# Attention and a SiLU MLP in one kernel: w_in loaded on all partitions, one K in another tag's buffer, a new hand-planned order

## The chip, the cores and the metric

The kernel runs on one core of a Trainium2 chip. The metric is the device time of one execution in microseconds (us). Five runs of the kernel before took 404.73 to 410.91, with a median of 405.35.

Engines are named as the profile names them: PE is TensorE (matmuls; PEld its weight loads), ACT is ScalarE, DVE is VectorE, POOL is GpSimd and SP is SyncE. Here POOL issues all loads, which also turn float32 into float16, and SP and ACT issue the stores.

## The reference

Softmax attention over 8 batches of 12 heads, 448 tokens and 64 dims, and then a two-layer MLP over its 3584 x 768 output:

```python
scores = scale * np.matmul(q, k.transpose(0, 1, 3, 2))
attn = softmax(scores)
attn_out = np.matmul(attn, v)                       # (B, H, S, D)
x = attn_out.transpose(0, 2, 1, 3).reshape(B * S, H * D)
h = x @ w_in                                        # 768 -> 2048
g = h * (1.0 / (1.0 + np.exp(-h)))
return g @ w_out                                    # 2048 -> 768
```

Inputs and output are float32 in DRAM.

## The kernel before

**Units of attention.** A unit is one batch and four heads; batch 0 is cut in two pieces of 224 queries, so that it makes units 0 to 5, and each later batch makes three. For a unit, `load_k` and `load_q` bring K and Q, DVE turns them in 32 x 32 blocks (`turn_k`, `turn_q`), PE computes scores (`s`), ACT takes the exponential (`E`), and PE computes three groups (`a`): the sums of the exponentials (part 0, with weights of ones) and two halves of the output (parts 1 and 2, with V as weights). DVE inverts the sums (`inverse`) and scales the halves into `xT` (`norm`). For most units DVE first adds the first three `E` tiles into a tile `T` (`add_e`), which shortens part 0.

**The MLP.** `ffn1` computes 128 rows of `h` (16 of them to a batch or piece) from six `xT` tiles and `w_in_t`. ACT takes the tanh (`th`), and DVE forms the gated value in `G` or `X` (`gate`). The second layer multiplies 2 x 2 blocks with seven products `p` (Strassen's scheme, with sums on DVE) for 13 "quads" of two 128-row tiles each; the first two tiles use 16 plain matmuls each (`o`). ACT and DVE read the products from PSUM into `ost`, and `store` writes each `ost` tile with four DMAs of 32 rows.

**The dims.** One block of an output half holds, for head `h` of the group, 32 of its 64 dims. Before, half 1 is dims 0 to 31 and half 2 is dims 32 to 63. Row `p` of a `w_in_t` block must hold the matching row of w_in, so `load_w_in` takes 32 partitions of three blocks at a time: 8 loads for each of three column ranges (512, 512 and 1024 columns), 24 in all.

**The order.** Nothing here is scheduled by a framework. The planner at the end of the kernel (`Order`, `Op`, `Ring`) plays through the work with estimated durations and then emits the instructions in that order; every engine runs its own queue in order. A `Ring` stands for a set of buffers: a step is planned only when one is free. On ACT and DVE the planner takes the waiting step with the least ready time plus `bias`, so that a lower bias goes first. On PE a burst of scores is taken when its time has come (`PACE` us after the last one) or when few MLP jobs are queued (`len(moe) < 6`); else an MLP job is taken, and attention groups when they are ready. While no MLP job has run yet, waits on PE are filled with matmuls of zeros (`z`, `run_zeros`).

**Loads.** They stand in POOL's queue in the order of the `plan_*` calls: K and Q of batch 0's three head groups, its V (4 loads), Q of units 3 to 5, the first two quarters of w_in, K and Q of unit 6, the last half of w_in, and so on. K tiles have two buffers (tag `rk`), Q tiles three (`rq`), `T` tiles two. So the third K waits until the first one has been turned.

**Splits.** In batch 0 a burst of scores holds two key chunks. For units below 6 it is split by pairs of heads into two half-bursts, each with its own exponential.

**The last stores.** In the last quad the odd ones of the four stores of a tile go to ACT's queue, but only for the tiles with `i == j` (L584).

Of the kernel before, what the change touches and what calls it, by code (L numbers as in the profile page):

```python
# [9 lines left out]
FP16 = mybir.dt.float16  # L10
# [154 lines left out]
def kernel(  # L165
# [9 lines left out]
    nc = tc.nc  # L175
# [4 lines left out]
    HG = 4  # L180
# [10 lines left out]
    NDC = DM // 128  # L191
    NT = 2 * S // 128
    OH = DM // 2
    PACE = 3
    LONE = NG + 1
    PIECES = ((0, 7), (7, TPP))
    NE, NXT = 9, 16
# [28 lines left out]
    def group_of(src, b, hg):  # L226
        return src[b, HG * hg : HG * (hg + 1)].rearrange("h (i g) d -> (h i) (g d)", g=TPP)

    def load_k(b, hg):
        t = sb.tile([128, TPP, D], FP16, name=f"rk_{b}_{hg}", tag="rk", bufs=2)  # L230
        nc.gpsimd.dma_start(out=t, in_=group_of(k, b, hg))  # L231
        rawk[(b, hg)] = t

# [10 lines left out]

    def load_v(b, hg0, hg1, x):
        if b not in VT:
            VT[b] = sb.tile([128, NH, NCH, D], FP16, name=f"V_{b}", tag="V", bufs=2)
        hs = slice(HG * hg0, HG * hg1)
        first, count = X_TOK[form(b, hg0)][x]
        nc.gpsimd.dma_start(  # L250
            out=VT[b][32 * x : 32 * (x + 1), hs, 0:count, :],
            in_=v[b, hs].rearrange("h (i g) d -> i h g d", g=TPP)[
                :, :, first : first + count, :
            ],
        )


    def load_w_in(h, j, f0, f1):
        src = moe_w_in.rearrange("(c h j p) f -> h j p c f", h=HG, j=2, p=32)
        dst = w_in_t.rearrange("p (c j) f -> p j c f", j=2)  # L260
        nc.gpsimd.dma_start(
            out=dst[32 * h : 32 * (h + 1), j, :, f0:f1], in_=src[h, j, :, :, f0:f1]
        )

    def load_w_out(f0, f1, m0, m1):
# [101 lines left out]
    def attend_mm(a, n, part, c, h, k0, k1, e, start, stop):  # L367
        b, hg, g0, g1 = units[n]
        nq = 32 * (g1 - g0)
        at = nq * (c % per_burst(n))  # L370
        if part == 0:
            w = ones[k0:k1, :]
        else:
            w = VT[b][k0:k1, HG * hg + h, c, 32 * (part - 1) : 32 * part]
        nc.tensor.matmul(  # L375
            out=a[32 * h : 32 * (h + 1), 0:nq],
            lhsT=w,
            rhs=e[k0:k1, h, at : at + nq],
            start=start,
            stop=stop,  # L380
        )
# [193 lines left out]
    def store(qd, i, j):  # L575
        u, t = divmod(2 * qd + i, NT)
        for w in range(4):
            r, col = divmod(128 * t + 32 * w, S)
            b = 2 * u + r
            dst = out[b * S : (b + 1) * S, OH * j : OH * (j + 1)].rearrange(  # L580
                "(i g) m -> g i m", g=TPP
            )

            eng = nc.scalar if w % 2 and 4 * qd + 4 == NT * B and i == j else nc.sync  # L584
            eng.dma_start(
                out=dst[col // 32], in_=ost_t[(qd, i, j)][32 * w : 32 * (w + 1), :]
            )
# [43 lines left out]
    od = Order()  # L631
    s_ring, m_ring, e_ring = Ring(2), Ring(4), Ring(NE)
    th_ring, tmp_ring, ost_ring = Ring(3), {3: Ring(2), 1: Ring(1)}, Ring(NOST)
    rk_ring, rq_ring, v_ring = Ring(2), Ring(NRQ), Ring(2)
    kt_ring, qt_ring = Ring(3), Ring(3)
    ld_k, ld_q, ld_v, ld_win, ld_wout = {}, {}, {}, {}, {}
# [2 lines left out]
    MB = 1e-6 * 4 * 32 * HG * D  # L639

    def plan_k(b, hg):
        ld_k[(b, hg)] = od.load(1.2 * MB * TPP, lambda: load_k(b, hg), rk_ring)

    def plan_q(n):
        ld_q[n] = od.load(1.2 * MB * (units[n][3] - units[n][2]), lambda: load_q(n), rq_ring)
# [9 lines left out]

    def plan_w_in(f0, f1):
        made = [
            od.load(4e-6 * (125 if f1 - f0 < DFF // 2 else 96) * (f1 - f0), lambda h=h, j=j: load_w_in(h, j, f0, f1))
            for h in range(HG)
            for j in range(2)  # L660
        ]
        for f in range(f0 // 128, f1 // 128):
            ld_win[f] = made
# [49 lines left out]
    def plan_turn(n):  # L713
        b, hg, g0, g1 = units[n]
        if (b, hg) not in kt_op:
            if not kt_ring.can(1, od.now):
                return False
            kt_ring.take()
            op = Op("DVE", 0.72, lambda: turn_k(b, hg), [ld_k[(b, hg)]], 20)
            op.then = rk_ring.give  # L720
            kt_op[(b, hg)] = od.add(op)
        if not qt_ring.can(1, od.now):
            return False
        qt_ring.take()
        busy = 0.1 + (g1 - g0) * 32 / 960.0
        qt_op[n] = od.add(
            Op("DVE", busy, lambda: turn_q(n), [ld_q[n]], 20, then=rq_ring.give)
        )
        return True
# [9 lines left out]
    def queue_ffn1(b, g0, g1):  # L739
        t0, t1 = 32 * g0, 32 * g1  # L740
        for f in range(NFF) if b == 0 else [x for f in range(HF) for x in (f, f + HF)]:

            def run(f=f):
                op = Op("PE", NDC * mm(t1 - t0), lambda: ffn1(b, f, t0, t1), tail=PE_OUT)
                if warm["on"]:
                    warm["on"] = False
                    m_ring.give(od.now)
                m_ring.take()
                od.on_pe(op, "full")
                th = od.add(  # L750
                    Op("ACT", act(t1 - t0), lambda: tanh(b, f, t0, t1), [op], -2, tail=0.2, ring=th_ring)
                )
                g = Op(
                    "DVE",
                    (t1 - t0) / 960.0 + 0.13,
                    lambda: gate(b, f, t0, t1),
                    [th],
                    -1,
                    then=lambda at: (m_ring.give(at), th_ring.give(at)),
                )  # L760
                g_op.setdefault((b, f), []).append(od.add(g))
                ffn1_left[b] -= 1

            def deps(f=f):
                made = [(x_op[(b, cc, g0)], cc * mm(t1 - t0)) for cc in range(NDC)] + ld_win[f]

                u, r = divmod(b, 2)
                for qd in range(NT * B // 4) if u else ():
                    if any(t // NT == u - 1 and (r or t % NT < 4) for t in (2 * qd, 2 * qd + 1)):
                        made += (  # L770
                            [plain_op.get(x) for x in ((0, 0), (0, 1), (1, 0), (1, 1))]
                            if qd == 0
                            else [pr_op.get((qd, m)) for m in (3, 4, 6, 7)]
                        )
                return made

            moe.append((deps, 1, run))
            ffn1_left[b] += 1

    def sums_w(ms):  # L780

        for m in ms:
            w_op[m] = [
                od.add(
                    Op(
                        "DVE",
                        0.9,
                        lambda m=m, f0=f0: combine_w(m, f0, f0 + 4),
                        ld_wout[0] + ld_wout[1] + list(plain_op.values()) * (m in (3, 7)),
                        100,  # L790
                    )
                )
                for f0 in (0, 4)
            ]

    def queue_plain(t, j):
        def run():
# [7 lines left out]
                    act(OH),  # L805
                    lambda: take_plain(t, j),
                    [op],
                    -0.3,
                    then=lambda at: (m_ring.give(at), ost_ring.give(at + STORED)),
                    ring=ost_ring,  # L810
                )
# [16 lines left out]
    def plan_sums():  # L828
# [12 lines left out]
        for m in (5, 2, 1, 6, 7):  # L841
            sg_op[(qd, m)] = []
            for f0 in (0, 4):
                deps = [x for f in range(f0, f0 + 4) for x in gates[f] + gates[f + HF]]
                if m > 5:
# [5 lines left out]
                            0.34,  # L851
                            lambda m=m, f0=f0: combine_g(qd, m, f0, f0 + 4),
                            deps,
                            8,
                        )
                    )
                )
# [1 line left out]
    def queue_quad(qd):  # L859
# [2 lines left out]

        def read(m, eng, fn, deps, *free):
            busy = act(OH) if eng == "ACT" else OH / 960.0 + 0.13
            bias = -0.3 if eng == "ACT" else -1
            ring = tmp_ring[m] if m in tmp_ring else ost_ring if m in (2, 5, 6, 7) else None

            def then(at):
                for r in free:
                    r.give(at)  # L870
                if ring is ost_ring:
                    ring.give(at + STORED)

            took[m] = od.add(Op(eng, busy, lambda: fn(qd), deps, bias, then=then, ring=ring))
# [86 lines left out]
    qk_seq, av_seq = [], []  # L961
    for ns in jobs:
        if len(ns) == 1:
            split = ((0,), (1,)) if ns[0] < 6 else ((0, 1),)
            qk_seq += [(ns, c, ys) for c in range(NCH // per_burst(ns[0])) for ys in split]
        else:
            qk_seq += [([n], c, (0, 1)) for n in ns for c in range(NCH - 1)]
            qk_seq.append((ns, 3, (0, 1)))
        av_seq += [(ns, part) for part in range(3)]
    e_adds, t_op, t_ring = [], {}, Ring(NTS)  # L970
    pace = {"next": 0.0}
    av_data = {"at": None}

# [56 lines left out]
    def plan_e():  # L1030
        while e_adds:
            n, c = e_adds[0]
            if c == 1:
# [3 lines left out]
            e_adds.pop(0)  # L1037
            deps = exp_op[n][: 2 * c + 2] + t_op.get(n, [])
            t_op[n] = [
                od.add(Op("DVE", HG * S / 1920.0 + 0.1, lambda n=n, c=c: add_e(n, c), deps, 0))  # L1040
            ]

    def av_at():
# [65 lines left out]
    def after_av(n, part, op, nq):  # L1109
        b, hg, g0, g1 = units[n]  # L1110
        if part == 0:
            made = []
            before = ([op] + inv_op[-1:], [], norm_op[-4:])
            for step, busy in enumerate((nq / 960.0 + 0.15, 0.2, nq / 960.0 + 0.15)):
# [2 lines left out]
                    busy,  # L1117
                    lambda step=step: inverse(n, step),
                    made[-1:] + before[step],
                    -10,  # L1120
                )
                made.append(od.add(r))
            made[0].then = m_ring.give
# [2 lines left out]
        else:  # L1126
# [2 lines left out]
                nq / 960.0 + 0.13,  # L1129
                lambda: norm(n, part),  # L1130
                [op] + rdn_op[n],
                -10,
                then=m_ring.give,
            )
            x_op[(b, 2 * hg + part - 1, g0)] = od.add(x)
# [17 lines left out]
    while True:  # L1153
# [4 lines left out]
        if od.free["PE"] <= od.now:  # L1158
# [6 lines left out]
                moe_i, moe_next = moe_ready(0)  # L1165
                soon.append(min([x for x in m_ring.free if x>od.now] or [od.now+0.1]))
            if qk is not None and qk <= od.now and (
                od.now >= pace["next"] or moe_i is None or len(moe) < 6
            ):
                u0 = units[qk_seq[0][0][0]]  # L1170
                pace["next"] = min(max(pace["next"], od.now - 4), od.now) + PACE * len(qk_seq[0][2]) / 2
# [61 lines left out]
```

The softmax here doesn't subtract the row's maximum and nothing guards it: scores larger than these inputs give would overflow.

## Time and profile before

| what | value |
|---|---|
| median of 5 runs | 405.35 us |
| profiled execution | 410.91 us, its span 409.1 us |
| mean granted PE clock | 0.977 |
| PE / DVE / ACT / POOL busy | 400.7 / 299.3 / 234.2 / 95.9 us |
| loads of w_in: POOL issue time | 13.4 us for 24, mean 566 ns |
| w_in loads of 96 KB / 192 KB, issue to landing | 4.4 / 7.8 us |
| scores: matmuls, mean | 864, 352 ns |
| exponentials: count, mean | 172, 914 ns |
| stores issued by SP / ACT | 220 / 4 |

How to read it: busy times are those of one execution on the profiler's clock, and a busy PE is not PE at its peak, since matmuls overlap. The span runs from the first to the last instruction; the time of the execution holds a little more. The clock row of the page gives the granted PE clock in tenths for 40 slices of the span. The duration that a timeline gives for a group runs to the end of its last matmul, so what PE needs for it is better read from one start to the next.

### The profile page before, as it was taken

The page shows a single profiled execution, that of the slowest core. Times are in us where ns is not written, and L with a number is a line of the kernel's source. Part 1 is how long each engine was busy: PE and PEld are TensorE (multiplying, and loading weights), DVE is VectorE, ACT ScalarE, POOL GpSimd, SP SyncE. Part 2 cuts the span into 40 slices and gives each one's busy share as a digit, 9 for nine tenths or more (in the row PEclk, how much of TensorE's full clock was granted, in tenths as well). Part 3 has the DMA queues.
Part 4 walks back from the last instruction along what each step waited for, and adds up shares of the span by engine and source line. Part 5 has one row for each costly group of instructions (what it writes and reads, how often), then busy time and mean ns, then how long its engine had stood idle before and what let it go on. Part 6 is the DMA issues. An engine that isn't in the chain of part 4 may idle for free.

```text
span 409.1 us, 9442 instructions
## 1 busy us (share of the span) xinstructions
PE 400.7 (98%) x3767; PEld 206.1 (50%) x3767; DVE 299.3 (73%) x646; ACT 234.2 (57%) x360; POOL 95.9 (23%) x175
## 2 busy tenths in 40 slices
PE   8999999999999999999999999999999999999994
PEld 7667674444454444444446444444445444555562
DVE  2436675999988887697698769778698667685763
ACT  3557887587565775652981296665781473223410
POOL 6776383454000813140000431521000000000000
PEclk9569999999999999999999999999999999999999
DMA  7999999694312971684001592635002300131014
GB/s 103 173 156 205 199 143 204 114 151 63 53 38 60 138 125 21 100 123 116 2 2 39 103 174 45 84 62 94 0 7 50 97 6 2 26 83 48 2 47 107
DMA packets 38747, 34.43 MB, mean 84 GB/s; under 512 B 11952, under 2 KB 37936, under 8 KB 38704
## 3 DMA queue, kind: packets, MB, share of 16 engines
q0 software_dynamic: 27952, 22.82, 38.8%
q1 hardware_dynamic: 10560, 10.83, 10.3%
q8 instruction: 29, 0.48, 0.5%
q10 hardware_dynamic: 192, 0.20, 0.2%
q14 instruction: 14, 0.11, 0.1%
HBM read 45.61 MB, written 11.01 MB: 138 GB/s over the span
## 4 chain that ended last, share of the span: by engine, by line
PE 96%; DVE 1%; ACT 1%; issue 0%; ACTq 0%
PE h L446 37%; PE p L537 29%; PE s L311 13%; PE a L375 12%; PE o L551 3%; PE z L1148 2%; ACT E L348 1%; DVE T L359 1%; DVE rdn L424 0%; DVE ost L590 0%; DVE sT L415 0%; DVE G L493 0%; DVE X L493 0%; DVE inv L421 0%; DVE zeros L214 0%
## 5 line engine op out<-in xcount | busy, mean ns | idle before, releaser
L348 ACT ACTIVATE E<-s 128x896 f16<-128x896 f32 (+1 forms) x172 | 149.5, 914 | 53.7 <-PE s L311 52.7
L446 PE MATMUL h<-xT,w_in_t 128*128 128x448 f16 (+1 forms) x864 | 157.8, 332 | 0.1
L446 PEld LDWEIGHTS <-w_in_t 128*128 128x128 f16 x864 | 79.2, 98 | 72.7 <-issue 19.4
L457 ACT ACTIVATE th<-h 128x448 f16<-128x448 f32 (+1 forms) x144 | 71.7, 505 | 58.1 <-PE h L446 53.4
L493 DVE SCALAR_TENSOR_TENSOR G<-th,h 128x448 f16<-128x448 f16 (+2 forms) x144 | 74.8, 532 | 35.7 <-ACT th L457 33.8
L250 POOL DMA_DIRECT2D V<-in_v_dram x88 | 48.5, 559 | 122.5 <-PE a L375 105.2
L311 PE MATMUL s<-QT,KT 32*128 32x448 f16 (+4 forms) x864 | 59.6, 352 | 0.4 <-ACT E L348 0.4
L537 PEld LDWEIGHTS <-G 128*128 128x128 f16 x384 | 36.7, 98 | 28.5 <-issue 4.6
L375 PE MATMUL a<-E,V 128*32 128x448 f16 (+3 forms) x864 | 42.5, 349 | 0.0
L537 PEld LDWEIGHTS <-S 128*128 128x128 f16 x312 | 29.5, 98 | 22.8 <-issue 4.3
L537 PE MATMUL p<-D,G 128*128 128x384 f16 x208 | 37.8, 326 | 0.5 <-DVE sT L415 0.5
L537 PE MATMUL p<-w_out_t,S 128*128 128x384 f16 x208 | 36.8, 326 | 0.0
L432 DVE SCALAR_TENSOR_TENSOR xT<-a,rdn 128x448 f16<-128x448 f32 (+1 forms) x54 | 28.9, 562 | 9.1 <-PE a L375 8.7
L311 PEld LDWEIGHTS <-KT 32*128 32x128 f16 (+2 forms) x864 | 18.9, 103 | 29.2 <-issue 28.0
L537 PE MATMUL p<-w_out_t,G 128*128 128x384 f16 x176 | 31.8, 326 | 0.0
L375 PEld LDWEIGHTS <-V 128*32 128x32 f16 (+2 forms) x864 | 19.2, 99 | 23.5 <-issue 16.1
L359 DVE TENSOR_TENSOR T<-E,E 128x1792 f16<-128x1792 f16 x20 | 21.7, 1087 | 11.4 <-ACT E L348 11.4
L527 DVE TENSOR_TENSOR S<-G 128x512 f16<-128x512 f16 x70 | 26.5, 417 | 4.3 <-PE p L537 4.2
L359 DVE TENSOR_TENSOR T<-T,E 128x1792 f16<-128x1792 f16 x20 | 21.7, 1085 | 8.8 <-ACT E L348 8.8
L231 POOL DMA_DIRECT2D rk<-in_k_dram x24 | 13.5, 562 | 50.0 <-DVE KT L285 43.6
L285 DVE STREAM_TRANSPOSE KT<-rk 128x256 f32<-128x256 f32 (+3 forms) x48 | 16.6, 383 | 9.2 <-DMA rk<-in_k_dram 8.3
L600 ACT COPY ost<-p 128x384 f32<-128x384 f32 x13 | 6.3, 482 | 24.4 <-PE p L537 24.4
(41 smaller groups left out, 270.6 us busy)
## 6 DMA issues: line engine op xcount, KB each, us to landing
out_dram<-ost SPq DMA_DIRECT2D x220, 48.0 KB, 1.6
rk<-in_k_dram POOLq DMA_DIRECT2D x24, 224.0 KB, 5.0
rq<-in_q_dram POOLq DMA_DIRECT2D x21, 224.0 KB, 5.6
w_out_t<-in_moe_w_out_dram POOLq DMA_DIRECT2D x8, 384.0 KB, 8.7
V<-in_v_dram POOLq DMA_DIRECT2D x43, 64.0 KB, 4.6
V<-in_v_dram POOLq DMA_DIRECT2D x40, 48.0 KB, 4.0
w_in_t<-in_moe_w_in_dram POOLq DMA_DIRECT2D x16, 96.0 KB, 4.4
w_in_t<-in_moe_w_in_dram POOLq DMA_DIRECT2D x8, 192.0 KB, 7.8
```

Source lines behind the costliest of these rows:

```text
L250: nc.gpsimd.dma_start(out=VT[b][32 * x : 32 * (x + 1), hs, 0:count, :], in_=v[b, hs].rearrange("h (i g) d -> i h g d", g=TPP)[:, :, first ...
L285: nc.vector.transpose(out=turned.rearrange("p c x i -> p x c i")[:, x:y, 0:count], in_=t[:, first : first + count * (y - x)].rearrange("p ...
L311: nc.tensor.matmul(out=pS[p0 : p0 + 32 * (x1 - x0), h % 2, at : at + nq], lhsT=KT[(b, hg)][32 * h : 32 * (h + 1), c, x0:x1, :, e], rhs=QT[ ...
L348: nc.scalar.activation(out=E[(n, w)][0:kr, 2 * y : 2 * y + 2, 0:nk], in_=pS_t[(n, w, y)][0:kr, :, 0:nk], func=AF.Exp, scale=attn_scale,)
L359: nc.vector.tensor_tensor(out=T_t[n], in0=E[(n, 0)] if c == 1 else T_t[n], in1=E[(n, c)], op=ALU.add,)
L375: nc.tensor.matmul(out=a[32 * h : 32 * (h + 1), 0:nq], lhsT=w, rhs=e[k0:k1, h, at : at + nq], start=start, stop=stop,)
L432: nc.vector.scalar_tensor_tensor(out=xT[(b, cc)][:, 32 * g0 : 32 * g1], in0=acc[(n, part)][:, 0:nq], scalar=0.5, in1=rdn_t[n].rearrange("p ...
L446: nc.tensor.matmul(out=h[:, 0 : t1 - t0], lhsT=w_in_t[:, cc, 128 * f : 128 * (f + 1)], rhs=xT[(b, cc)][:, t0:t1], start=(cc == 0), stop=(c ...
L457: nc.scalar.activation(out=th, in_=h_t[(b, f, t0)][:, 0 : t1 - t0], func=AF.Tanh)
L493: nc.vector.scalar_tensor_tensor(out=dst[:, f, at + lo : at + hi], in0=th_t[(b, f, t0)][:, lo - t0 : hi - t0], scalar=1.0, in1=h_t[(b, f, ...
L527: nc.vector.tensor_tensor(out=dst[:, f0:f1], in0=x[:, f0:f1], in1=y[:, f0:f1], op=op)
L537: nc.tensor.matmul(out=pr_t[(qd, BANK[m])][:, 0:OH], lhsT=w[:, f, :], rhs=W_[m][:, f, :], start=(f == 0 and BANK[m] == m), stop=(f == HF - 1),
```

## The change

- `V`'s tile and the two output halves: half 1 is now the even dims of a head and half 2 the odd ones. The weights of parts 1 and 2 are read from V with a step of two elements.
- With that, partition `p` of two neighbouring `w_in_t` blocks holds rows `2p` and `2p + 1` of w_in, and `load_w_in` fills all 128 partitions of two blocks: 3 loads for each column range, 9 in all.
- K of batch 0's third head group is loaded into a buffer of tag `T`, and its ring follows.
- The order: `PACE` from 3 to 3.4; scores go first while fewer than 30 MLP jobs are queued (6 before); unit 5 isn't split; biases of `gate`, `combine_w`, the PSUM reads, `combine_g`, `add_e`, `inverse` and `norm` are new.
- In the last quad the odd stores of all four tiles go to ACT.

```diff
-    PACE = 3
+    PACE = 3.4
     def load_k(b, hg):
-        t = sb.tile([128, TPP, D], FP16, name=f"rk_{b}_{hg}", tag="rk", bufs=2)
+        if (b, hg) == (0, 2):
+            t = sb.tile([128, HG, S], FP16, name=f"rk_{b}_{hg}", tag="T", bufs=NTS)
+            t = t.rearrange("p h s -> p (h s)")[:, 0 : TPP * D]
+            t = t.rearrange("p (g d) -> p g d", d=D)
+        else:
+            t = sb.tile([128, TPP, D], FP16, name=f"rk_{b}_{hg}", tag="rk", bufs=2)
...
-            VT[b] = sb.tile([128, NH, NCH, D], FP16, name=f"V_{b}", tag="V", bufs=2)
+            VT[b] = sb.tile([128, NH, NCH, D // 2, 2], FP16, name=f"V_{b}", tag="V", bufs=2)
...
-    def load_w_in(h, j, f0, f1):
-        src = moe_w_in.rearrange("(c h j p) f -> h j p c f", h=HG, j=2, p=32)
-        dst = w_in_t.rearrange("p (c j) f -> p j c f", j=2)
+    def load_w_in(hg, f0, f1):
+        src = moe_w_in.rearrange("(c p j) f -> c p j f", p=128, j=2)
         nc.gpsimd.dma_start(
-            out=dst[32 * h : 32 * (h + 1), j, :, f0:f1], in_=src[h, j, :, :, f0:f1]
+            out=w_in_t[:, 2 * hg : 2 * hg + 2, f0:f1], in_=src[hg, :, :, f0:f1]
         )
...
-            w = VT[b][k0:k1, HG * hg + h, c, 32 * (part - 1) : 32 * part]
+            w = VT[b][k0:k1, HG * hg + h, c, :, part - 1]
...
-            eng = nc.scalar if w % 2 and 4 * qd + 4 == NT * B and i == j else nc.sync
+            eng = nc.scalar if w % 2 and 4 * qd + 4 == NT * B else nc.sync
...
-            od.load(4e-6 * (125 if f1 - f0 < DFF // 2 else 96) * (f1 - f0), lambda h=h, j=j: load_w_in(h, j, f0, f1))
-            for h in range(HG)
-            for j in range(2)
+            od.load(4e-6 * 256 * (f1 - f0), lambda hg=hg: load_w_in(hg, f0, f1))
+            for hg in range(NG)
...
                     lambda: gate(b, f, t0, t1),
                     [th],
-                    -1,
+                    -0.3,
...
-                        100,
+                        30,
...
                     lambda: take_plain(t, j),
                     [op],
-                    -0.3,
+                    -2,
...
                             lambda m=m, f0=f0: combine_g(qd, m, f0, f0 + 4),
                             deps,
-                            8,
+                            0,
...
-            bias = -0.3 if eng == "ACT" else -1
+            bias = -2 if eng == "ACT" else -4
...
-            split = ((0,), (1,)) if ns[0] < 6 else ((0, 1),)
+            split = ((0,), (1,)) if ns[0] < 5 else ((0, 1),)
...
                     lambda step=step: inverse(n, step),
                     made[-1:] + before[step],
-                    -10,
+                    -1,
...
                 lambda: norm(n, part),
                 [op] + rdn_op[n],
-                -10,
+                -1,
...
-                od.now >= pace["next"] or moe_i is None or len(moe) < 6
+                od.now >= pace["next"] or moe_i is None or len(moe) < 30
```

More of the change, by code (lines that the diff above doesn't have):

```diff
@@ L250, in load_v @@
         nc.gpsimd.dma_start(
-            out=VT[b][32 * x : 32 * (x + 1), hs, 0:count, :],
+            out=VT[b].rearrange("p h c i e -> p h c (i e)")[
+                32 * x : 32 * (x + 1), hs, 0:count
+            ],
             in_=v[b, hs].rearrange("h (i g) d -> i h g d", g=TPP)[
@@ L633 @@
     th_ring, tmp_ring, ost_ring = Ring(3), {3: Ring(2), 1: Ring(1)}, Ring(NOST)
+    t_ring = Ring(NTS)
     rk_ring, rq_ring, v_ring = Ring(2), Ring(NRQ), Ring(2)
@@ L641, in plan_k @@
     def plan_k(b, hg):
-        ld_k[(b, hg)] = od.load(1.2 * MB * TPP, lambda: load_k(b, hg), rk_ring)
+        ring = t_ring if (b, hg) == (0, 2) else rk_ring
+        ld_k[(b, hg)] = od.load(1.2 * MB * TPP, lambda: load_k(b, hg), ring)
     def plan_q(n):
@@ L719, in plan_turn @@
             op = Op("DVE", 0.72, lambda: turn_k(b, hg), [ld_k[(b, hg)]], 20)
-            op.then = rk_ring.give
+            op.then = (t_ring if (b, hg) == (0, 2) else rk_ring).give
             kt_op[(b, hg)] = od.add(op)
@@ L969 @@
         av_seq += [(ns, part) for part in range(3)]
-    e_adds, t_op, t_ring = [], {}, Ring(NTS)
+    e_adds, t_op = [], {}
     pace = {"next": 0.0}
@@ L1039, in plan_e @@
             t_op[n] = [
-                od.add(Op("DVE", HG * S / 1920.0 + 0.1, lambda n=n, c=c: add_e(n, c), deps, 0))
+                od.add(Op("DVE", HG * S / 1920.0 + 0.1, lambda n=n, c=c: add_e(n, c), deps, -1))
             ]
```

## The prediction

> **What bounds the kernel now.** I read the page first, then the chain of waits, the table of stages, the timelines of POOL and PE at the start, and those of SP, ACT and DVE at the end. From the page:
>
> ```profile
> PE 400.7 (98%) x3767; PEld 206.1 (50%) x3767; DVE 299.3 (73%) x646; ACT 234.2 (57%) x360; POOL 95.9 (23%) x175
> ...
> PEclk9569999999999999999999999999999999999999
> ...
> PE h L446 37%; PE p L537 29%; PE s L311 13%; PE a L375 12%; PE o L551 3%; PE z L1148 2%; ACT E L348 1%; DVE T L359 1%; DVE rdn L424 0%; DVE ost L590 0%; DVE sT L415 0%; DVE G L493 0%; DVE X L493 0%; DVE inv L421 0%; DVE zeros L214 0%
> ```
>
> TensorE is the bound nearly everywhere, and two slices ran on a lowered clock. Which stage has slack is in the table of stages (two answers; time, then PE, PEld, DVE, ACT, POOL busy, clock, DMA share, GB/s):
>
> ```profile
> 11.57:28.64 17.07, 17.07 (x233) 10.77 (x234) 7.04 (x21) 8.74 (x11) 13.53 (x25) 0.50 1.17 163
> 28.64:45.00 16.36, 15.75 (x287) 11.46 (x288) 9.12 (x27) 12.89 (x21) 8.62 (x15) 1.00 1.19 205
> ```
> ```profile
> 120.00:345.00 225.00, 224.34 (x2024) 102.99 (x2022) 179.47 (x369) 136.04 (x202) 38.20 (x70) 1.00 0.37 66
> ```
>
> From 28.6 us PE never stops for long: of the 225 us of the middle it idles 0.66. What an order can still save there is only changes of the PE's tiling: in the chain 84 `h` in a row take 15.89 us (189 ns each), twelve between score bursts 2.38 (198 each), so a change costs about 0.1 us. The middle is therefore a floor, and I look for the gain at both ends.
>
> The start on POOL (start, duration, what, idle before and releaser):
>
> ```profile
> 5.80 0.54 POOL L231 DMA_DIRECT2D rk<-in_k_dram  x1 [2.26 <-DVE QT L296]
> 6.33 0.54 POOL L237 DMA_DIRECT2D rq<-in_q_dram  x1
> 6.85 2.47 POOL L250 DMA_DIRECT2D V<-in_v_dram  x4
> 9.30 1.12 POOL L237 DMA_DIRECT2D rq<-in_q_dram  x2
> 12.56 0.54 POOL L237 DMA_DIRECT2D rq<-in_q_dram  x1 [2.14 <-DVE sT L415]
> 13.08 1.14 POOL L261 DMA_DIRECT2D w_in_t<-in_moe_w_in_dram  x2
> ...
> 15.61 6.22 POOL L261 DMA_DIRECT2D w_in_t<-in_moe_w_in_dram  x11 [0.47 <-DMA V<-in_v_dram]
> ```
>
> The third K stands 2.26 us at the head of POOL's queue for a buffer, and 24 w_in loads of 0.56 us follow. On PE meanwhile:
>
> ```profile
> 27.31 1.00 PE L311 MATMUL s<-QT,KT 32*96 32x224 f16 x16
> 28.25 0.79 PE L1148 MATMUL z<-zeros 128*128 128x128 f16 x8
> 28.87 0.74 PE L446 MATMUL h<-xT,w_in_t 128*128 128x224 f16 x6
> 29.54 0.57 PE L311 MATMUL s<-QT,KT 32*128 32x224 f16 x8
> ```
>
> The first useful filler, `h`, starts at 28.87. The eight zero matmuls just ahead are the planner's filler for a wait it expected. The end on SP, ACT and DVE:
>
> ```profile
> 397.44 5.42 SPq L585 DMA_DIRECT2D out_dram<-ost  x12
> ```
> ```profile
> 403.83 3.18 SPq L585 DMA_DIRECT2D out_dram<-ost  x6
> ```
> ```profile
> 403.20 1.79 ACTq L585 DMA_DIRECT2D out_dram<-ost  x4
> ```
> ```profile
> 403.43 0.56 DVE L590 TENSOR_TENSOR ost<-p,s 128x384 f32<-128x384 f32 x1 [0.26 <-PE p L537]
> ```
>
> The last tile is ready at 403.99, but SP issues stores (about 0.46 us each) without a break of more than 1 us from 397.44 to 407.01: its queue, not the arithmetic, sets the end.
>
> [...] The trace has no w_in load on all partitions; its 32-partition ones took 4.4 us (96 KB) to land.
>
> **How the profiled run stands to the median.** It took 410.91 (span 409.1, 1.8 around it), 5.56 over the median of 405.35. The half clock explains this: in those 17.07 us lie 11 half-bursts of scores (0.50 each start to start at full clock, from 29.54 on), some 9 groups of 16 `a` (0.44) and 23 zero matmuls (0.056): 5.5 + 4.0 + 1.3 = 10.8, so 6.3 us at most. I take it that the median run has no such stretch; there `h` starts near 28.87 - 6.1 = 22.8.
>
> **The change, part by part.**
>
> *End: stores of the last quad on two queues.* Now 4 of its 16 go to ACT, then 8. SP has 4 fewer of about 0.47 us: 1.9 us. SP would end its issues at 407.0 - 1.9 = 405.1, ACT as now at 405.0, both just after the last tile (403.99), so no more than 2.0 is to be had. ACT's four extra stores stand behind its copies at 396.9 and 399.5; nothing else runs on ACT there until 403.2, so nobody waits. Value -1.9, bounds -1.2 to -2.1[...].
>
> *Unit 5 not split.* [...]a burst of four costs PE what one of two does: at 7.13 us the PE timeline has two halves back to back, 16 matmuls in 0.59 us, where a lone half of 8 takes 0.57. Unit 5's four lone halves (35 to 41 us) become two bursts: 2 x 0.50 less, of which I take -0.95. PE is full there, so it counts. Bounds -0.7 to -1.1.
>
> *Third K into a `T` buffer, and w_in in 9 loads.* POOL loses the 2.26 us wait, so K, its Q, V (landing 6.3 to 7.3 us after issue) and the next Q come about 2.2 us earlier. 15 issues of 0.56 us go: 8.4 us of POOL, 5 x 0.56 = 2.8 of them in the first quarter of w_in. `T` is first written for real at 59.6 us, so borrowing it costs nothing. In the median run `h` at about 22.8 stands right where w_in allows it: its eighth load was issued at 17.94 and lands 4.4 to 4.8 later, 22.3 to 22.7. With the change three loads leave at about 11 to 12.5, and bytes become the bound: three K, six Q, V and the quarter are 2.85 MB; at the present rate (73, 132, 158, 184 GB/s in the four 5-us stretches) that is 20.7 us, with the earlier issue some 20.5. ScalarE allows not much sooner: twelve exponentials of 0.86 from 7.75 are 18.1, plus three `a` groups and a norm, about 20.2. So `h` starts 2.3 us earlier, less one half-burst of scores (0.50) not yet done by then: -1.8. Bounds: 0 (with PE at half clock it is its own bound) to -2.4. A w_in load of all partitions is not in the trace: issue between K's 0.56 (128 runs) and w_out's 0.75 us, I take 0.6; 9 x 0.6 is 5.4 against 13.4.
> The later halves of w_in and batch 1 also land earlier. No wait of PE or DVE for a DMA is in the trace after 16.5, so nothing is gained.
>
> *V's weights with a step of two.* All 864 weight loads from V change. KT's are read so already: 95 ns for 128 columns against 98 for w_in's contiguous ones. Zero; V's runs in the DMA stay whole. Bounds 0 to +0.3 us, as weight loads overlap.
>
> *Order (PACE, backlog 30, biases).* Scores go ahead of MoE work until 30 jobs are queued, then one burst in 3.4 us. The work is the same, the bursts fewer by two, and the middle has 0.66 us of idle to give. Two waits, 0.61 at 41 us and 0.53 at 184, may go or come elsewhere. Norms lose their first place on VectorE to reads of PSUM; `h` of that batch waits for them, but PE has a backlog. Value 0, bounds -1.5 to +2.
>
> Sum: -1.9 - 0.95 - 1.8 = -4.65: 405.35 to **400.7** (in the profiled run's terms 410.9 to 406.3 at most, less if the half clock stays).
>
> **Rivals.**
> *Half clock in most runs.* [...]where clock drops as in the profile the time is 400.7 + 5.6 = 406.3, above the median of before. It decides once the drop costs more than 4.65 us[...]. For: two of five runs shown lie at 410. Against: the other three don't[...].
> *w_in isn't what holds `h`.* If scores and norms are as late as now, the start gives nothing: 405.35 - 2.85 = 402.5.
> *VectorE becomes the bound.* The front of attention is crowded: a pair of units costs DVE 4 x 1.09 (T) + 2 x 1.3 (turns) + 2 x 1.5 (inverse) + 4 x 0.61 (norm), 12.4 us, and PE only about 7.5. From 90 to 100 us DVE is already busy 9.8 of 10 us. If running attention ahead makes gates late, PE's four PSUM banks fill: 1.3 us a pair is 13 us over ten pairs, 405.35 - 4.65 + 13 = 413.7. It decides above 4.65 us of new PE waits. Against: total DVE 179 of 225 in the middle leaves room, and scores throttle themselves on DVE's turns.
>
> **How the numbers follow.** Forecast 62%, half clock 17%, w_in not the bound 14%, VectorE 7%. A measurement tells about 1% here, 4.05 us: faster is below 401.3. Three quarters of the forecast's chance lie there (its own range 399.0 to 402.2): faster 0.47, slower 0.07, the rest, 0.46, within 1%. The range to 406.5 takes in the half clock and leaves VectorE out.
>
> **What would show it.** Right: POOL without the 2.26 us wait, nine w_in issues; `h` at 20 to 21.5 us at full clock; SP's last store issued within 1.5 us of DVE's last `ost`; PE idle in the middle under 2 us. Wrong: clock 0.50 for over 10 us at the start, `h` no earlier at full clock, PE waits for `G`, `X` or `ost` between 60 and 345, or SP still issuing 2 us after the last tile.

## The result, and the profile after

The changed kernel takes 403.75 us (median of 43 executions, 402.65 to 409.19) against 405.17 for the kernel before in the same measurement. The ratio is 0.9964, with a 95% interval of 0.9949 to 0.998: 0.2 to 0.5% faster, where the forecast had 1.15%. Every kernel here has executions with a mean granted TensorE clock under 0.996 (the profiled ones of before and after were at 0.50, "half clock" below, for 17.07 and 13.65 us of the start), so I also give medians "at full clock", over the executions with a mean of 0.996 or more: 403.52 for the change, 404.9 to 405.2 for the kernel before. The limit lets in 1.6 us of lost clock, 0.004 of a span of about 405 us: as much as the profile of `b_loads` lost from 28.64 to 45 us, where its mean is 0.90 (16.36 x 0.10). Differences below are between those unless a ratio stands there.

The profiled execution after is one with such a stretch (408.57 us, span 406.8). From its page:

```profile
PE 397.4 (98%) x3758; PEld 204.3 (50%) x3758; DVE 301.8 (74%) x646; ACT 234.4 (58%) x360; POOL 88.8 (22%) x160
...
PEclk9759999999999999999999999999999999999998
```

POOL lost 7.1 us of busy time, PE 3.3. The table of stages of the changed kernel, with the columns of before:

```profile
11.57:28.64 17.07, 16.27 (x240) 10.61 (x234) 6.24 (x18) 9.72 (x13) 11.09 (x17) 0.60 1.22 194
...
120.00:345.00 225.00, 224.55 (x1970) 104.45 (x1968) 177.91 (x363) 132.37 (x198) 38.21 (x70) 1.00 0.38 67
```

The middle idles 0.45 us instead of 0.66: neither gain nor harm there. The half clock lasts 13.65 us (0.50 from 14.97 to 28.62) instead of 17.07: the mean over the 17.07 us is 0.60 instead of 0.50, so 1.7 us less of lost clock. POOL's timeline at the start:

```profile
3.51 0.57 POOL L237 DMA_DIRECT2D rk<-in_k_dram  x1
...
4.55 2.52 POOL L256 DMA_DIRECT2D V<-in_v_dram  x4
...
11.91 2.11 POOL L269 DMA_DIRECT2D w_in_t<-in_moe_w_in_dram  x3
```

The third K no longer waits, V is issued 2.3 us earlier, and a load of w_in on all partitions costs 0.70 us to issue. On PE:

```profile
14.99 0.94 PE L383 MATMUL a<-E,V 128*32 128x224 f16 x16 [0.80 <-DMA V<-in_v_dram]
...
26.79 2.18 PE L454 MATMUL h<-xT,w_in_t 128*128 128x224 f16 x12
```

PE waits 0.80 us for V, and `h` starts at 26.79, at a clock of 0.50. The end, on SP and DVE:

```profile
389.39 14.91 SPq L593 DMA_DIRECT2D out_dram<-ost  x24
```
```profile
401.89 0.56 DVE L598 TENSOR_TENSOR ost<-p,s 128x384 f32<-128x384 f32 x1 [0.26 <-PE p L545]
```

The last tile is ready at 402.45 and SP's last issue ends at 404.30: 1.85 us later, where it was 3.0 before.

### The profile page after: what moved, and what is told of

The parts are those of the page before. It is cut to its first block, busy times and chain, and to the rows that moved or that the text cites. A ratio compares the mean times of both kernels' runs of the same rounds, so it can differ in the third digit from the quotient of the medians.

```text
span 406.8 us, 9398 instructions
## 1 busy us (share of the span) xinstructions
PE 397.4 (98%) x3758; PEld 204.3 (50%) x3758; DVE 301.8 (74%) x646; ACT 234.4 (58%) x360; POOL 88.8 (22%) x160
## 4 chain that ended last, share of the span: by engine, by line
PE 92%; DMA 2%; DVE 2%; POOL 1%; ACT 1%; issue 1%; DVEq 0%; POOLq 0%
PE h L454 36%; PE p L545 30%; PE a L383 12%; PE s L319 11%; PE o L559 3%; DMA V<-in_v_dram 2%; ACT E L356 1%; DVE T L367 1%; POOL rk L237 0%; POOL rq L243 0%; DVE G L535 0%; DVE xT L440 0%; POOL V L256 0%; DVE ost L598 0%; PE z L1157 0%
## 5 line engine op out<-in xcount | busy, mean ns | idle before, releaser
L454 PEld LDWEIGHTS <-w_in_t 128*128 128x128 f16 x864 | 80.5, 98 | 70.9 <-issue 16.5
L319 PE MATMUL s<-QT,KT 32*128 32x448 f16 (+4 forms) x864 | 56.6, 348 | 1.2 <-ACT E L356 1.2
L319 PEld LDWEIGHTS <-KT 32*128 32x128 f16 (+2 forms) x864 | 17.2, 102 | 29.2 <-issue 28.1
L535 DVE TENSOR_TENSOR S<-G 128x512 f16<-128x512 f16 x70 | 25.2, 416 | 0.7 <-PE p L545 0.7
L423 DVE STREAM_TRANSPOSE sT<-a 128x448 f32<-128x448 f32 (+1 forms) x27 | 15.8, 587 | 5.1 <-PE a L383 4.7
```

The lines of the kernel that those rows point to most:

```text
L319: nc.tensor.matmul(out=pS[p0 : p0 + 32 * (x1 - x0), h % 2, at : at + nq], lhsT=KT[(b, hg)][32 * h : 32 * (h + 1), c, x0:x1, :, e], rhs=QT[ ...
L454: nc.tensor.matmul(out=h[:, 0 : t1 - t0], lhsT=w_in_t[:, cc, 128 * f : 128 * (f + 1)], rhs=xT[(b, cc)][:, t0:t1], start=(cc == 0), stop=(c ...
L535: nc.vector.tensor_tensor(out=dst[:, f0:f1], in0=x[:, f0:f1], in1=y[:, f0:f1], op=op)
```

## Experiments

In the labels `a_` is the changed kernel with an edit, `b_` the kernel before with one. Theory at first: the parts add up as forecast, and a part that brought little was hidden. Rivals: `h` is held by something else than w_in; the new order costs what the loads bring.

### The end: stores

`a_store_old` undoes the store rule, `b_store_new` does it alone.

```diff
-            eng = nc.scalar if w % 2 and 4 * qd + 4 == NT * B else nc.sync
+            eng = nc.scalar if w % 2 and 4 * qd + 4 == NT * B and i == j else nc.sync
```

> The changed kernel with the old rule for the last quad's stores (ACT takes odd stores only of the tiles with i == j); nothing else differs on any engine. Forecast's step: +1.9 us against the changed kernel. Theory now, from the two profiles (end of the last matmul to end of the span 5.74 us before, 4.95 after): +0.8[...]. Rival: 0, the end gives nothing in undisturbed runs.

> The kernel before with the new rule for the last quad's stores alone; PE, DVE and POOL as before. Forecast's step: -1.9 us against the kernel before. Theory now ([...]the same edit taken back in the changed kernel cost 1.1): -1.1. Its start is that of the kernel before: where the clock is full, theory now expects the first h at 22 to 23 us, released by VectorE's norm and not by w_in; the forecast's step expects it at 22.8, released by w_in.

Measured: `a_store_old` 404.65 at full clock, 1.13 over the change (ratio to before 1.0019, 0.9986 to 1.0052). `b_store_new` 403.33 (0.9967, 0.9945 to 0.9989), 1.6 under before. So the store rule alone gives as much as the whole change. From the end of the last matmul to the end of the span it is 5.74 us before, 4.02 in `b_store_new`, 6.1 in `a_store_old` and 4.95 after.

`a_store2` goes one quad further:

```diff
-            eng = nc.scalar if w % 2 and 4 * qd + 4 == NT * B else nc.sync
+            eng = nc.scalar if w % 2 and 4 * qd + 8 >= NT * B else nc.sync
```

> The changed kernel with odd stores of the last two quads on ACT, not of the last one only; PE, DVE and POOL the same. Theory now (the last stores wait in SP's queue[...]): SP is free some 1.8 us sooner before the last two tiles, -0.5 to -1.0 us. Rival (the landing of the last store, about 1.6 us, is all that is left): 0 to -0.2.

Measured: 402.67, 0.85 under the change (0.9971, 0.9942 to 1.0001). SP's timeline in `a_store2` and, for comparison, the row above:

```profile
384.62 13.61 SPq L593 DMA_DIRECT2D out_dram<-ost  x15
```

SP's run ends at 398.23 and ACT's at 398.34, 1.5 us after the last matmul (396.7), against 2.5 in the changed kernel (404.30 against 401.85). In the changed kernel SP's queue was therefore still the last thing to end: ACT's stores there ended at 403.42, 0.9 before SP's.

### The split of unit 5

`a_split6` splits it again, `b_split5` unsplits it in the kernel before.

```diff
-            split = ((0,), (1,)) if ns[0] < 5 else ((0, 1),)
+            split = ((0,), (1,)) if ns[0] < 6 else ((0, 1),)
```

> The changed kernel with unit 5 split in half-bursts as before (planned anew from there on). Forecast's step: +0.95 us against the changed kernel (two lone half-bursts of 0.50 us more on a full PE). Rival: under +0.3, because a planned order that starts elsewhere gives and takes as much.

> The kernel before with unit 5 unsplit alone (planned anew from there on). Forecast's step: -0.95 us against the kernel before. Theory now (two bursts of about 0.5 us less; taking it back in the changed kernel cost 1.7, so the plan behind it gives or takes up to 1 us): -0.3 to -1.7. Rival (with the old order it costs, as the old order with the new loads and unit 5 unsplit was slow): +0.3 to +1.5.

Measured: `a_split6` 405.24, 1.7 over the change (ratio to before 1.003, 1.0002 to 1.0059). `b_split5` 404.56, only 0.4 under before (0.9985, 0.9966 to 1.0005, so by itself not clear of noise). Why so little shows in PE's timeline. `b_store_new`, where unit 5 is still split:

```profile
33.44 0.60 PE L311 MATMUL s<-QT,KT 32*96 32x224 f16 x8
...
36.25 0.37 PE L375 MATMUL a<-E,ones 96*32 96x224 f16 x6 [0.61 <-ACT E L348]
```

and `b_split5`:

```profile
33.72 0.61 PE L311 MATMUL s<-QT,KT 32*96 32x224 f16 x16
...
35.33 0.27 PE L375 MATMUL a<-E,ones 96*32 96x224 f16 x2 [0.69 <-ACT E L348]
36.13 0.37 PE L375 MATMUL a<-E,ones 96*32 96x224 f16 x6 [0.53 <-ACT E L348]
```

The two half-bursts of 8 (the other at 34.64) are one burst of 16 in the time of 8, but the sums that follow wait 0.69 + 0.53 = 1.22 us for ACT's exponentials instead of 0.61. PE saves about 0.95 in all and gives 0.61 back, so 0.35 is left, about what was measured. From the first `h` (23.28 us in `b_store_new`, 23.48 in `b_split5`) to the `h` that begins at 39.87 and 39.75, PE indeed needs 0.32 us less.

The 1.7 us of `a_split6` are another matter. Its profile has 1.65 us of PE idle from 120 to 345 us, far behind unit 5, where the change has 0.45: the planner's later order is worse there, with one wait of 0.65 us for a sum on DVE at 128 us and three shorter ones for DVE.

### The start: loads

`b_loads` takes the three changes of loads alone into the kernel before (V even and odd, w_in in 9 loads, the third K in a `T` buffer), as the diff of the change shows them.

> The kernel before with the loads alone: V in even and odd dims, w_in in 9 loads, the third K in a T buffer; old order values, old split, old stores. Forecast's step: -1.8 us against the kernel before. Theory now: 0 to -0.5, as V comes only about 1 us earlier and w_in isn't what holds the first h.

Measured: 406.46, 1.4 *over* before (1.0044, 1.0022 to 1.0067). `a_v_by_group` instead loads batch 0's V in twelve parts, the first head group's ahead of the rest:

```diff
-    plan_v(0, 0, NG)
+    for hg in range(NG):
+        plan_v(0, hg, hg + 1)
```

> The changed kernel with V of batch 0 loaded by head group (12 smaller loads, not 4), so that the first group's V lands some 2 to 3 us earlier; planned anew. Theory now (PE stands 0.8 us before the first V group and ScalarE idles behind it): -0.5 to -1.2 us against the changed kernel. Rival (V is not on the path, or eight more issues of 0.56 us cost as much): 0 to +1.

Measured: 404.80, 1.3 over the change (1.0042, 1.0014 to 1.0071). PE no longer waits for V, but for w_in. Its timeline, where `h` begins at 22.02 and then stops twice:

```profile
23.30 0.37 PE L454 MATMUL h<-xT,w_in_t 128*128 128x224 f16 x2 [0.92 <-DMA w_in_t<-in_moe_w_in_dram]
24.57 0.94 PE L454 MATMUL h<-xT,w_in_t 128*128 128x224 f16 x8 [0.90 <-DMA w_in_t<-in_moe_w_in_dram]
```

Eight more V issues, with two waits of POOL between them (1.56 and 0.74 us, for landings of K), put w_in's first issue from 11.6 to 15.15 us, and the wait goes over to it. So with V out of the way, w_in comes next.

What does hold `h`? Two profiles at full clock (1.00 from 5 to 25 us) show the start of each kernel. `b_store_new` has the start of before; its chain of waits there (start, duration, what):

```profile
6.12 0.53 POOL rk L231
...
8.39 7.11 DMA V<-in_v_dram
...
16.37 1.34 PE a L375 x48
...
23.44 0.57 PE h L446 x6
```

and `a_store_old` has the start of after, here the chain and then PE's loads of weights:

```profile
14.66 0.43 issue
15.10 0.57 PE a L383 x16
...
22.75 1.26 PE h L454 x12
```
```profile
15.06 0.34 PEld L383 LDWEIGHTS <-V 128*32 128x32 f16 x16 [0.66 <-DMA V<-in_v_dram]
```

No w_in stands in the chain of before: it ran over the third K's buffer and V. The chain of after runs on PE alone and books the wait ahead of the first value group as 0.43 us of "issue", but the weights of that group were waiting for V. From the landing of V PE then goes on to `h`, with one stop of 0.24 us in `a_store_old` (at 21.57) and none in `b_store_new`. The loads of w_in that `h` needs (those of the first column range) had landed by then: the last of its eight at 21.98 us in `b_store_new`, 1.3 ahead of `h` (23.28), and the last of its three at 20.28 in `a_store_old`, 2.4 ahead (22.68).

With the change V's four loads are out at 7.07 instead of 9.64 us, but the first matmul on V comes only 1.27 us earlier (15.10 against 16.37). The last V load took 8.6 us to land instead of 7.3, in a stretch (5 to 25 us) where the table of stages has a DMA share of 1.23 against 1.09, and 190 against 152 GB/s. From there PE's chain is 7.65 us after and 7.07 before: the difference is mainly one half-burst of scores more (0.50, which the forecast had counted) and the stop. So `h` comes 0.7 us earlier in the chains (0.60 in the timelines, 22.68 against 23.28).

Two runs that were to price single parts can't. `a_w36` cuts each load of w_in in four of 32 partitions; `a_krk` puts the third K back in `rk`, each with the plan unchanged:

```diff
-            out=w_in_t[:, 2 * hg : 2 * hg + 2, f0:f1], in_=src[hg, :, :, f0:f1]
+                out=w_in_t[p : p + 32, 2 * hg : 2 * hg + 2, f0:f1],
+                in_=src[hg, p : p + 32, :, f0:f1],
...
-        if (b, hg) == (0, 2):
+        if False:
```

> The changed kernel with each w_in load cut into four of 32 partitions (36 loads, not 9); the planner doesn't know of it, so the order on PE, ACT and DVE is the same, and POOL issues 27 more loads of about 0.56 us. Forecast's step (w_in holds the first h): +1.8 us or more against the changed kernel. Theory now (the first h is held by V and what follows from it, not by w_in): +0.0 to +0.3.

> The changed kernel with the third K back in its own tag's two buffers; the order on all engines is the same, POOL waits about 2.2 us for the buffer again, so V and w_in are issued 2.2 us later. Theory now (PE stands before the first V group; DMA engines are full, so V lands only about 1 us later): +0.5 to +1.2 us against the changed kernel. Rival (the start has slack enough for it): 0 to +0.2.

Measured: `a_w36` 408.11 (six executions, 1.0079, 1.0065 to 1.0093), `a_krk` 408.8 (six, 1.0081, 1.0051 to 1.011). Five of the six of `a_w36` and all six of `a_krk` fall short of full clock, and the sixth lies at the limit itself (means 0.983 to 0.996, and 0.980 to 0.989), where the changed kernel has 33 of 44 at full clock. At a mean clock of 0.986 or less `a_w36` (407.89, one execution) and `a_krk` (409.06, five) are within 0.8 of the change (408.64, eight), and PE never waits for w_in in `a_w36`'s profile; `a_krk`'s shows 1.6 us of wait for V instead of 0.8. For `a_w36` the clock can't be all of it: its three executions at 0.995 and 0.996 took 407.58 to 408.6, at least 4.1 over the change, while their lost clock is 0.004 to 0.005 of a span of 406 us, 1.6 to 2.0. No profile shows where the other 2.4 or more went. In the one there is, at a mean clock of 0.983, the first quarter of w_in has landed by 21.96, but POOL issues the K of unit 6 at 25.42 instead of 16.86. So neither run says what its part costs at full clock.

### The order

`a_order_old` puts all of the old order back under the new loads; `a_pace_old` only its two numbers; `a_bias_old` only its biases.

```diff
-    PACE = 3.4
+    PACE = 3
...
-                od.now >= pace["next"] or moe_i is None or len(moe) < 30
+                od.now >= pace["next"] or moe_i is None or len(moe) < 6
```

> The changed kernel with the order's old values: PACE 3, backlog 6, and all old biases; loads, third K, stores and unsplit unit 5 stay. Theory now (the middle is full PE either way, the new order is worth nothing): within 0.3 us of the changed kernel. Rival A (the new order spends what the start gains): 1 to 2 us faster than the changed kernel. Rival B (the new order is where the gain is): 0.5 us or more slower.

> The changed kernel with PACE 3 and backlog 6, its biases kept. Theory P (the order's 3 us come from scores going ahead while the backlog is under 30): +2.5 to +3.5 us against the changed kernel. Theory B (they come from the biases, which put reads of PSUM and norms in another order on VectorE): 0 to +0.7.

> The changed kernel with the old biases, its PACE 3.4 and backlog 30 kept. Theory P (pace and backlog give the order's 3 us): 0 to +0.7 us against the changed kernel. Theory B (the biases do): +2.5 to +3.5.

Measured: `a_order_old` 406.71 (1.0037, 1.0013 to 1.0061), `a_pace_old` 405.95 (1.0029, 1.0016 to 1.0042), `a_bias_old` 403.37 (0.9976, 0.9959 to 0.9994). With the new pace the biases are worth nothing, with the old one perhaps 0.8 (`a_pace_old` against `a_order_old`); the pace is worth 2.4 us on the new loads.

Is it worth that by itself? `b_pace_new` puts the new pace into the kernel before, `b_two` has the new stores and the unsplit unit 5 alone, and `b_two_pace` all three.

> The kernel before with the new pace alone (3.4 and at most 30 waiting steps instead of 3 and 6), its loads, its split, its stores and its biases kept: the corner of the square loads by pace that is still missing. Theory (the new pace only repairs what the new loads upset in the old order, the stall of `h` behind the weight sums at 75 to 85 us): no gain on the old loads, 404.5 to 406. Rival (the pace is worth its 2.4 us with either loads, and the new loads then cost 1.4 with either pace): 402.6.

> The kernel before with the new store rule and unit 5 unsplit, its loads and its order kept. Theory (the two edits add, and the loads with the new order bring nothing beyond them): 405.0 - 1.6 - 0.4 = 403.0, 0.5 below the whole change. Rival (the loads and the order carry part of the gain of the whole change, the stores overlapping with the unsplit unit): 404.0 or more.

> The kernel before with the new store rule, unit 5 unsplit and the new pace: the whole change less its loads and its biases. Theory (loads and pace cancel only together): as with the old pace or up to 1 us slower, 403.0 to 404.0. Rival (pace worth 2.4 with either loads): 400.6. Against the whole change at 403.5 this gives the worth of the loads under the new pace: 0 to -0.5 by the theory, +2.9 (slower) by the rival.

Measured: `b_pace_new` 405.26 (1.0004, 0.9984 to 1.0023): no gain, as the theory had it. `b_two` 403.12 (0.9943, 0.9925 to 0.996): the two edits add (2.0 under before), and they alone are 0.4 faster than the whole change at full clock, little more than the 0.3 by which the kernel before differs between measurements. One of its executions took 496.5 us at a mean clock of 0.753; its profile is of that one, and nothing is read from it. `b_two_pace` 407.38 (1.0057, 1.003 to 1.0085): far worse than either expectation, and scattered (404.76 to 408.76 at full clock, and one execution of 778.17 us, which hardly moves the median: 407.17 without it). With the new stores, unit 5 unsplit and the old biases, at full clock:

| | pace 3, backlog 6 | pace 3.4, backlog 30 |
|---|---|---|
| loads of before | 403.12 (`b_two`) | 407.38 (`b_two_pace`) |
| loads of the change | 406.71 (`a_order_old`) | 403.37 (`a_bias_old`) |

The new loads cost 3.6 us with the old pace, the new pace 4.3 with the old loads, and both together 0.25. Of the two bad corners many executions lie at 0.996, where 1.6 us of lost clock fits. Over 0.997 or more they read 407.03 (8 executions) and 405.94 (4), so that the sizes are 3.9 and 2.8; the signs stay.

It isn't a matter of these two alone. With unit 5 split and the old stores, the new pace costs 0.1 on the old loads (`b_pace_new`), and the new loads 1.4 on the old pace (`b_loads`). So the split, or the stores, has a part in it too; no run separates them.

What is it in the order? The table of stages from 75 to 85 us, where batch 1's attention hands over to its MLP: one fence each for `b_store_new`, the changed kernel, `b_loads` and `b_two_pace`, in this order:

```profile
75.00:85.00 10.00, 10.00 (x94) 4.23 (x91) 9.42 (x20) 8.84 (x14) 5.03 (x10) 1.00 1.14 176
```
```profile
75.00:85.00 10.00, 9.73 (x113) 4.16 (x106) 9.66 (x21) 6.24 (x9) 4.74 (x9) 1.00 0.94 145
```
```profile
75.00:85.00 10.00, 8.57 (x93) 3.07 (x94) 10.00 (x21) 6.97 (x10) 5.42 (x10) 1.00 0.70 106
```
```profile
75.00:85.00 10.00, 8.32 (x126) 2.85 (x126) 10.00 (x20) 7.04 (x9) 3.95 (x8) 1.00 0.87 140
```

The second number after the stretch is PE's busy time, the fourth DVE's: PE is full or nearly so in the good plans (in `b_pace_new` too, 10.00) and idles 1.4 to 1.7 us of 10 in the bad ones (`a_pace_old` has 8.56; `a_order_old` 9.08, with 0.52 more of idle from 85 to 90), while DVE is full or nearly so. PE's timeline of `b_loads`:

```profile
75.25 0.57 PE L319 MATMUL s<-QT,KT 32*128 32x448 f16 x8
...
77.12 1.06 PE L383 MATMUL a<-E,V 128*32 128x448 f16 x20 [0.62 <-DVE sT L423]
...
79.82 0.35 PE L454 MATMUL h<-xT,w_in_t 128*128 128x448 f16 x1 [0.45 <-DVE xT L440]
```

Between the two value groups (the first ends as the scores at 75.25 begin) stands this one burst and nothing else, so PE runs into DVE's chain from the sums to `xT`. In the good plans a group of 16 `o` (2.77 us) stands there to cover it; in the bad ones all of them have been used up earlier. `b_loads_o` brings it back through a pace that goes the other way, with the loads of `b_loads`:

```diff
-    PACE = 3
+    PACE = 2.95
```

> The kernel before with the three changes of loads and the pace 2.95 instead of 3, everything else of the order kept. In TensorE's order this moves one group of 16 matmuls `o` (2.77 us) of batch 0 from ahead of the first value matmuls of the last unit to between its two groups of value matmuls, where the kernel before and the changed kernel have it, and the slower plans not. Theory (that group covers the chain from the sums over `xT` to the first `h` of the next batch, whose waits were 0.62 + 0.45 + 0.18 + 0.18 = 1.43 us with the loads at pace 3): 406.46 - 1.43 = 405.0. Rival (a longer pace is what helps, 3.4 and 30 being worth 2.4): 406.3 or more, since this pace goes the other way.

PE's timeline there, and its row of the table:

```profile
74.22 2.77 PE L559 MATMUL o<-w_out_t,G 128*128 128x384 f16 x16
76.92 1.63 PE L383 MATMUL a<-E,V 128*32 128x448 f16 x32
...
79.00 1.31 PE L454 MATMUL h<-xT,w_in_t 128*128 128x448 f16 x6
```
```profile
75.00:85.00 10.00, 9.73 (x91) 4.10 (x89) 9.58 (x19) 6.99 (x11) 5.06 (x10) 1.00 0.87 135
```

The waits are gone as expected, 1.16 us of PE's idle time with them. But the time is 406.27 (1.0051, 1.0025 to 1.0077), 0.2 under `b_loads` and not 1.4: the theory holds for the wait and fails for the time. In the profiles PE idles 0.50 us more from 60 to 75 us, in a wait for an exponential at 60.7 us, and 0.31 more from 7 to 30; by these stages about 0.35 of the 1.16 is left, and the spans differ by 0.3 (405.9 against 406.2). So this stall can't be shown to be what makes the loads slow: an order that fills one wait opens others.

### Best parts

`a_best` is the change with the old biases and the store rule of `a_store2`; `b_two_store2` is `b_two` with that store rule.

> The changed kernel with the old biases and the odd stores of the last two quads on ScalarE's queue. Theory (the biases are worth 0.15, the wider store rule 0.85, at different ends of the kernel): 402.5. Rival (both shorten the same tail after the last matmul, since the old biases also brought it from 4.95 to 4.38 us): 402.7 to 403.0.

> The kernel before with unit 5 unsplit and the odd stores of the last two quads on ScalarE's queue; its loads and order kept. Theory (the wider rule is worth 0.85 where the last quads follow each other as in the changed kernel, less here, where the new rule alone already brought the tail from 5.74 to 4.02 us against 4.95): 403.1 less 0 to 0.3. Rival (the wider rule is worth 0.85 here too): 402.3.

Measured: `a_best` 402.82 at full clock (0.9966, 0.9937 to 0.9994), `b_two_store2` 403.09 (0.9934, 0.9908 to 0.9959). Neither adds anything to its parts: in `a_best` the biases bring nothing beyond the stores, and with the old loads the wider rule brings 0.03 over `b_two`. At full clock `a_store2` (402.67) and `a_best` are the fastest measured; `b_two` and `b_two_store2` are within 0.5 of them and have the lower ratios to before, so which of the four is best isn't settled.

## Why the prediction was wrong

**Direction right, size three times too large**: -4.65 forecast, about -1.5 measured. By steps:

- *Stores, -1.9.* Right in mechanism: SP's queue ended last (its last issue ended 3.0 us after the last tile, 1.85 after the change), and four stores less on it gave -1.6 in the kernel before, within the bounds. In the change it is worth 1.13, just outside them. The forecast asked for SP's last store within 1.5 us of the last `ost`, and it is issued 1.4 us after.
- *Unit 5, -0.95.* The saving on PE came, and 0.61 of it returned as a longer wait for the exponential: -0.4 by itself. The failed half-sentence is "PE is full there, so it counts". PE was full, yet next to a wait of 0.61 us in the same place (36.25 us, in the fence above). Undone in the change it costs 1.7, more than its own saving, so an interaction with the plan is in that number: 1.2 us of it shows as more idle time of PE between 120 and 345 us.
- *Third K and w_in, -1.8.* This is the step that failed. It rested on "`h` at about 22.8 stands right where w_in allows it". That the times agreed was an accident of reading w_in's landing in a profile at half clock and `h` in an imagined run at full clock. In a profile of that start at full clock (`b_store_new`) the eighth load lands at 21.98 and `h` begins at 23.28; the chain has no w_in in it, but K's buffer, V, and 7 us of PE without a stop. The second half of the error is that V was taken to land 2.2 us earlier when issued 2.2 us earlier: of the 2.6 us measured at the issue, half went into slower landings (8.6 us instead of 7.3, at a DMA share of 1.23 instead of 1.09), and 0.6 into a longer PE chain. `h` came 0.6 us earlier, not 2.3, and on the old pace the loads made the kernel 1.4 us slower. The rival "w_in isn't what holds `h`" named this (402.5), at 14%, and still expected a start worth nothing rather than a loss.
- *Order, 0.* Right as the sum of a bad and a good effect, wrong as a statement about the parts: loads and order together give +0.4 or nothing, the pace -2.4 on the new loads and +4.3 on the old. The forecast priced loads and order one by one, though the planner derives the order from the loads' due times. Its bounds (-1.5 to +2) hold neither the -2.4 nor the +4.3.
- *V's step of two, 0*, wasn't run alone.

So the sum reads -1.6 - 0.4 (which `b_two` confirms at -2.0) and +0.4 for loads and order: -1.6, against -1.5 measured. The expected gain of the start went to V's landing and to PE's own chain. Part of what was left is lost at the end: under the old store rule PE's last matmul ends at 396.88 us in `a_store_old` and at 397.75 in `b_split5`, 0.9 earlier with the new loads and order, but the tail behind it is 6.10 us instead of 5.75; under the new rule it is 4.95 instead of 4.02. So some of what PE saves is lost behind the last matmul; why the tail is longer wasn't traced.

The other rivals didn't decide. A lowered clock (a mean under 0.996) is in 11 of the change's 44 executions, not in the median; no run shows what lowers it. VectorE wasn't the bound of the middle (0.45 us of PE idle in 225), though it is what PE runs into at 75 to 85 us in the bad plans.

**What stays open.** Which waits make up the 1.4 us of `b_loads` once the stall at 75 to 85 us is covered: its profile has a mean clock of 0.90 from 28.64 to 45 us, and so has that of `b_loads_o`, so no full-clock trace of either was seen. What in the plans makes the worth of loads, pace and split depend on each other: the stall at 75 to 85 us marks the bad plans, but to cover it brought 0.2 us. And why three plans had a lowered clock in all or most executions, and two more, `b_loads` and `b_loads_o`, in 14 and 13 of 22.

## What to carry to other kernels

Before crediting an earlier load, follow the chain back from the instruction that is to come earlier, in a profile without a disturbed clock; that two times agree doesn't make one the cause of the other. In a kernel whose order comes from a planner, a change of load times is also a change of order: price both as one, look for the places where PE has just one block of work to cover a chain of VectorE, and check that this block is still there. And test the small, local edits alone: here one of them, the stores, gave as much as the whole change.

## What was not expected of the hardware

- How often the clock is lowered differs between plans. Means under 0.996 were in 5 of 6 executions of `a_w36`, 6 of 6 of `a_krk` and 17 of 22 of `a_v_by_group`, with three small changes of loads, against 11 of 44 of the change. It differs between measurements too: the kernel before had them in 14 of 40 executions measured with the first two and in 9 of 75 with the third, and `a_store_old`, the change with another store rule at its end, in 13 of 22. At means of 0.986 or less the change took about 5 us longer (408.64 against 403.52).
- A w_in load on all partitions (256 KB) took 0.70 us to issue and 6.9 to land, a 32-partition one (96 KB, the kernel before) 0.56 and 4.4: per KB the wide one cost POOL 2.7 ns against 5.8.
- A copy into `ost` can wait for a store. In `b_store_new` ACT's second copy of the last quad waits 2.12 us for an earlier store, where the changed kernel's same copy (at 396.95) waits 1.09 for PE.
